# One key-query product per head and chunk, transposed by VectorE and DMA, in a gated recurrence with a feed-forward layer behind it

## The chip, the cores and the metric

The kernel runs on one core of a Trainium2 chip. Its five engines follow their own instruction lists and wait for each other through semaphores: TensorE (PE, with its weight loads listed as PEld), VectorE (DVE), ScalarE (ACT), GpSimd (POOL) and SyncE (SP), which issues all DMAs here. The metric is the device time of one execution in microseconds (us).

## The reference

Four sequences of 768 steps have 8 heads of 48 channels. A complex gate decays and rotates a 48x48 state for each head, an outer product of key and value is added to its real part, and the query reads it. Heads are then joined to 384 columns, and a feed-forward layer with 2048 hidden columns follows. `w_in` and `w_out` come in float64, everything else in float32.

```python
mag = np.sqrt(a_re * a_re + a_im * a_im)
scale = np.minimum(mag, 0.999) / (mag + 1e-06)
a_re_n, a_im_n = (a_re * scale, a_im * scale)
for t in range(S):
    new_re = ar * S_re - ai * S_im
    new_im = ar * S_im + ai * S_re
    S_re, S_im = (new_re + kv, new_im)          # kv = k[t] outer v[t]
    y[:, :, t] = np.einsum('bhd,bhde->bhe', q[:, :, t], S_re)
...
h = x @ w_in                                     # x: y as (3072, 384)
g = h * (1.0 / (1.0 + np.exp(-h)))
return (g @ w_out)
```

In the inputs `a_re` lies between 0.85 and 0.95 and `a_im` is normal with a deviation of 0.1.

## The kernel before, in words

A gate is written as exp(l + 2 pi i th). With L and TH the running sums of l and th, step s reaches step t with the weight sum over d of q k exp(L[t]-L[s]) cos(TH[t]-TH[s]). Queries and keys are rotated by cos and sin (96 rows for 48 channels) and scaled by exp of sums of l, and a product of the two on TensorE gives the weights.

The sequences are cut into 24 chunks of 128 steps, two chunks to a pair, 12 pairs. The recurrence runs within a chunk in blocks of 64 steps, with a state carried from block to block. So that no scale can overflow, a block's weights come from several levels: `scales` (L341) makes six running sums of l for each head by two matmuls of 384 columns (`lt`), ACT turns them into `z` and `zk` by exp, `scaled` (L357) multiplies them with the transposed queries and keys on DVE, and `weights` (L401 to L418) takes products for the levels (`far`, `mid`, `near`) and puts them together through masks. `transposed` (L327) turns queries and keys by TensorE with copies by ACT and DVE, `state` (L383) updates the state once per block, `output` (L424, L428) reads values and states, and `tokens` (L442) turns the result for the feed-forward layer.

The gates of a pair come in `gates_log` and `gates_angle`: squares, logarithms, exponentials and an arctangent on ACT, with steps on DVE and POOL between. `trig` takes sine and cosine of the phases, and `phases` (L278, L280) sums the angles. These need three loads of ACT's function tables per pair, and `chain` keeps all functions on ACT in the order in which they are given.

The feed-forward layer of a pair of chunks has eight steps: `hidden` (L450, 6 products of 256 columns: h), tanh on ACT, a product on DVE (L455: g) and `result` (L465, 4 products of 384 columns: o). A float32 product appears as two MATMUL instructions in the trace. Weights in float64 are converted on DVE in pieces (L129 to L146) while the first pairs run.

The order of work: `attention(p)` gives the steps of a pair, `feed(p-1)` those of the feed-forward layer of the pair before, and `merge` interleaves the two lists. The tile framework then schedules each engine's list, within what its pools of buffers allow; PSUM has 2 banks for `lt` and `mid`, 3 for the rest of attention, 1 for h, 2 for o. After the last pair's attention one feed-forward layer runs alone.

## Time and profile before

| what | value |
|---|---|
| time of three runs | 1490.67 us median, 1480.78 to 1491.67 |
| span of the profiled execution (no device time of its own is listed; it lies 3.4 us above the median) | 1494.1 us |
| TensorE busy | 1341.6 us, 8592 matmul instructions |
| VectorE busy | 734.3 us |
| ScalarE busy | 487.3 us |
| GpSimd busy | 350.7 us |
| DMA packets | 136418, 42.27 MB |

A row of the groups names a line, an engine, an operation and its shape, then the count, the busy time, the mean duration of one (ns) and the idle time ahead of it with what ended it. A row of the timeline begins with its start and duration in us. A row of the stretches gives the stretch, its length, then busy time and count of PE, PEld, DVE, ACT and POOL, the granted clock of TensorE (1.00 is full), the share of DMA time and GB/s. TensorE's instructions overlap in the trace, so that a mean duration is longer than the spacing of a dense row.

### The profile page before, as it was taken

Reading aid. Unit: us, or ns where it says so; the run is one execution under the profiler, and the core shown is the slowest. Engines: PE = TensorE matmul, PEld = TensorE weight load, DVE = VectorE, ACT = ScalarE, POOL = GpSimd, SP = SyncE. Lnnn points to the kernel's source line nnn. Section 1 sums busy time; section 2 is a strip of 40 time slices with the busy share of each in tenths; the row PEclk is TensorE's granted clock in tenths of the full one; section 3 lists DMA queues with packets and bytes.
Section 4 is the critical chain, followed back from the end, with each engine's and each line's share of the span. In section 5 each row is a group of like instructions: output and inputs, shape, how many; then the busy total and the mean of one; then the engine's idle time right before and its main releaser. Section 6 shows DMA issues by size and latency. Waiting matters only on the chain. (4 is left out here: it accounts for less than half of the span.)

```text
span 1494.1 us, 21231 instructions
## 1 busy us (share of the span) xinstructions
PE 1341.6 (90%) x8592; PEld 937.5 (63%) x8592; DVE 734.3 (49%) x1592; ACT 487.3 (33%) x1009; POOL 350.7 (23%) x390
## 2 busy tenths in 40 slices
PE   1563798489999999999999999989999989999999
PEld 0342566256767666666766766756766756776676
DVE  4978778764444444444344444444344444334321
ACT  4433032303523513613523513513433513313301
POOL 5534011501322402301222311311131311301000
PEclk9975799789999999979999989979999999989979
DMA  5313111310020110110020110110010010000000
GB/s 121 85 50 90 41 43 54 75 37 6 17 49 1 32 33 1 31 29 6 13 52 1 29 36 0 28 32 6 6 38 1 12 30 3 6 12 1 1 11 11
DMA packets 136418, 42.27 MB, mean 28 GB/s; under 512 B 126080, under 2 KB 133248, under 8 KB 136320
## 3 DMA queue, kind: packets, MB, share of 16 engines
q1 hardware_dynamic: 136320, 40.91, 11.8%
q8 instruction: 68, 1.11, 0.3%
q14 instruction: 30, 0.25, 0.1%
HBM read 36.18 MB, written 4.72 MB: 27 GB/s over the span
## 5 line engine op out<-in xcount | busy, mean ns | idle before, releaser
L341 PE MATMUL lt<-sums,l 128*96 128x384 f32 x768 | 304.4, 518 | 46.5 <-DVE w L417 30.3
L465 PE MATMUL o<-w,g 128*128 128x384 f32 x768 | 282.2, 499 | 24.3 <-DVE w L146 24.3
L450 PE MATMUL h<-xT,w 128*128 128x256 f32 x1152 | 284.2, 392 | 18.1 <-DVE g L455 15.3
L450 PEld LDWEIGHTS h<-xT,w 128*128 128x128 f32 x1152 | 221.3, 196 | 78.1 <-DVE g L455 19.5
L220 ACT ACTIVATE z<-lt 96x384 f32<-96x384 f32 x384 | 187.2, 488 | 166.1 <-PE lt L341 164.3
L357 DVE TENSOR_TENSOR z<-z,qT 96x256 f32<-96x256 f32 (+1 forms) x288 | 149.4, 530 | 160.0 <-ACT z L220 159.1
L465 PEld LDWEIGHTS o<-w,g 128*128 128x128 f32 x768 | 145.8, 194 | 119.7 <-DVE w L146 27.2
L341 PEld LDWEIGHTS lt<-sums,l 128*96 128x96 f32 x768 | 126.8, 173 | 143.4 <-issue 64.1
L455 DVE SCALAR_TENSOR_TENSOR g<-tanh,h 128x512 f32<-128x512 f32 x96 | 65.3, 680 | 231.5 <-ACT tanh L220 231.5
L432 ACT COPY y<-y 128x192 f32<-128x192 f32 x48 | 15.3, 319 | 399.9 <-PE y L428 399.9
L220 ACT ACTIVATE tanh<-h 128x512 f32<-128x512 f32 x96 | 57.4, 598 | 249.2 <-PE h L450 223.5
L320 POOL TENSOR_TENSOR ks<-kr,es 128x384 f32<-128x384 f32 x48 | 47.5, 1009 | 326.3 <-ACT es L220 326.3
L387 POOL TENSOR_TENSOR S<-S,dec 96x192 f32<-96x192 f32 x88 | 56.1, 647 | 207.9 <-DVE S L390 205.6
L401 PE MATMUL far<-z 96*128 96x128 f32 x384 | 96.2, 334 | 0.1
L424 PE MATMUL y<-v,w 128*128 128x48 f32 x384 | 82.6, 299 | 9.4 <-DVE w L418 9.4
L352 POOL COPY dec<-z 96x8 f32<-96x8 f32 x48 | 32.8, 684 | 243.8 <-ACT z L220 243.8
L424 PEld LDWEIGHTS y<-v,w 128*128 128x128 f32 x384 | 64.0, 202 | 38.1 <-DVE w L418 23.8
L383 PEld LDWEIGHTS s<-v,ks 64*96 64x96 f32 x704 | 59.0, 170 | 41.0 <-issue 36.4
L357 DVE TENSOR_TENSOR z<-z,kT 96x256 f32<-96x256 f32 x192 | 79.7, 415 | 0.0
L410 PE MATMUL near<-z,zk 96*128 96x128 f32 x384 | 61.8, 313 | 14.4 <-DVE S L390 14.2
L300 POOL COPY l<-l 128x768 f32<-128x768 f32 x24 | 37.1, 1545 | 154.9 <-PE lt L341 153.0
L390 DVE TENSOR_TENSOR S<-s,S 96x192 f32<-96x192 f32 x88 | 30.9, 351 | 85.1 <-PE s L383 57.6
(92 smaller groups left out, 1685.2 us busy)
## 6 DMA issues: line engine op xcount, KB each, us to landing
raw<-in_moe_w_in_dram SPq DMA_DIRECT2D x24, 256.0 KB, 2.8
raw<-in_moe_w_out_dram SPq DMA_DIRECT2D x32, 192.0 KB, 2.4
re<-in_a_re_dram SPq DMA_DIRECT2D x24, 192.0 KB, 3.6
im<-in_a_im_dram SPq DMA_DIRECT2D x24, 192.0 KB, 3.3
k<-in_k_dram SPq DMA_DIRECT2D x24, 192.0 KB, 2.6
q<-in_q_dram SPq DMA_DIRECT2D x24, 192.0 KB, 2.7
v<-in_v_dram SPq DMA_DIRECT2D x24, 192.0 KB, 2.7
out_dram<-ot SPq DMA_DIRECT2D x24, 192.0 KB, 1.9
```

The costliest lines, as they stand in the source:

```text
L220: chain(nc.scalar.activation(out=out, in_=in_, func=func, **kw))
L320: nc.gpsimd.tensor_tensor(out=x["ks"][:, :, a], in0=x["kr"][:, :, a], in1=e, op=ALU.mult)
L341: nc.tensor.matmul(ps.rearrange("p s t -> p (s t)"), lhsT=two, rhs=sums[:, ts(g, NS // 2)].rearrange("p s t -> p (s t)"), start=True, stop ...
L357: eng.tensor_tensor(out=t, in0=t, in1=by, op=ALU.mult)
L383: nc.tensor.matmul(ps[:, h], lhsT=x["ks"][rows, hg].rearrange("p a d -> p (a d)"), rhs=x["v"][rows, hg], start=True, stop=True)
L387: nc.gpsimd.tensor_tensor(out=new, in0=x["S", i, hh], in1=x["dec", hh][:, :, ds(i, 1)].to_broadcast([D2, HH, D]), op=ALU.mult)
L401: nc.tensor.matmul(pf[:, h], lhsT=z[:, 2, h], rhs=z[:, 2, h], start=True, stop=True)
L410: nc.tensor.matmul(pn[:, h], lhsT=zk[:, h], rhs=z[:, 0, h], start=True, stop=True)
L424: nc.tensor.matmul(ps[:, h], lhsT=x["w", hh][:, h], rhs=x["v"][:, hh * HH + h], start=True, stop=False)
L450: nc.tensor.matmul(ps[:, ji], lhsT=w1[:, dc, ts(jp * 2 + ji, C)], rhs=A[p]["xT"][:, dc], start=(dc == 0), stop=(dc == ND - 1))
L455: nc.vector.scalar_tensor_tensor(out=g, in0=th, scalar=1.0, in1=ps, op0=ALU.add, op1=ALU.mult)
L465: nc.tensor.matmul(A[p]["o"][m], lhsT=A[p]["g", jp][:, ji, ts(m, C)], rhs=w2[:, j], start=(j == 0), stop=(j == NJ - 1))
```

## The change

The attention is rewritten. The decay of a step is counted from the head row of its chunk of 128: `decays` takes one running sum of l per chunk (a matmul of 384 columns), floors it at -60, and ACT gives exp(L) for queries (`eq`) and exp(-L) for keys (`ek`). `rotated` multiplies these into q and k on POOL and with cos and sin on DVE (`qk`). `turned` transposes on DVE in squares of 32x32 (`sq`), and 12 DMAs per chunk put the squares in their places (`T`; runs of 128 bytes). `weights` is then a single product per head (`a`) and one masked copy on DVE. The levels, their sums, `z`, the masks and TensorE's transposes are gone.

`state` works once per chunk instead of once per 64 steps; the decay over a chunk goes through DRAM (`ends`, `decs`). `output` gives y already transposed, with two heads in the two halves of PSUM's partitions; the last two heads are cut in thirds and sent to their rows by 6 DMAs per chunk (`xT`), for which the rows of `w_in` are permuted on loading. The pairs now go over sequences first (`place`): a pair holds the same chunk of two sequences, and the chunk it follows is two pairs back. Weight conversion uses 6 DVE instructions and a POOL product per piece instead of 9 on DVE, on pieces of 512 (`w_in`) and 384 (`w_out`) columns instead of 256 and 192, all of them listed ahead of the first feed-forward layer. h has 2 banks of PSUM.

For gates too strong for a single product a second path, `step_by_step`, runs the recurrence step by step and the feed-forward layer again. It is behind a branch that is taken when the smallest decay over a chunk is under 4e-18.

```diff
-    BL = 64
-    WC = 256
+    Q = 32
+    NB = D2 // Q
+    NA = C // Q
+    WC = 512
...
+    p_m = fast.enter_context(tc.tile_pool(name="p_m", bufs=2, space=PSUM))
+    p_a = fast.enter_context(tc.tile_pool(name="p_a", bufs=2, space=PSUM))
+    p_h = fast.enter_context(tc.tile_pool(name="p_h", bufs=2, space=PSUM))
+    p_o = fast.enter_context(tc.tile_pool(name="p_o", bufs=2, space=PSUM))
...
+    def place(n):
+        p, i = divmod(n, 2)
+        c, half = divmod(p, B // 2)
+        return 2 * half + i, c
...
+    def load_w1(cols, dc):
+        last = (H - 2) * D
+        third = D // ND
+        rows = [(0, 2 * dc * D, D), (D, last + third * dc, third),
+                (64, (2 * dc + 1) * D, D), (64 + D, last + D + third * dc, third)]
+        load_w(w1[:, dc, ts(cols, WC)], [(at, w_in[r:r + n, ts(cols, WC)]) for at, r, n in rows])
...
+        nc.gpsimd.tensor_tensor(out=x, in0=hi.bitcast(F32), in1=hi.bitcast(F32), op=ALU.mult)
...
+    decs = consts.tile([D2, N, H], F32)
+    ends = nc.dram_tensor("ends", (N, DM), F32).ap()
...
-        ps = bank([C, DM], f"phase{n}")
-        first = n % NCH == 0
-        nc.tensor.matmul(ps, lhsT=upto, rhs=cut(A[p]["th"], i), start=True, stop=first)
-        if not first:
-            nc.tensor.matmul(ps, lhsT=last, rhs=X[n - 1]["turn"], start=False, stop=True)
+        th = cut(A[p]["th"], i)
+        if place(n)[1] > 0:
+            carry = att.tile([1, DM], F32, tag="carry", name=f"carry{n}", bufs=1)
+            nc.sync.dma_start(out=carry, in_=X[before(n)]["turn"][C - 1:C])
+            nc.gpsimd.tensor_tensor(out=th[0:1], in0=th[0:1], in1=carry, op=ALU.add)
+        ps = p_m.tile([C, DM], F32, tag="m", name=f"phase{n}")
+        nc.tensor.matmul(ps, lhsT=upto, rhs=th, start=True, stop=True)
...
+    def decays(n):
...
+        ps = p_m.tile([C, DM], F32, tag="m", name=f"L{n}")
+        nc.tensor.matmul(ps, lhsT=upto, rhs=cut(A[p]["l"], i), start=True, stop=True)
+        L = att.tile([C, DM], F32, tag="whole", name=f"L{n}", bufs=1)
+        nc.vector.tensor_scalar(out=L, in0=ps, scalar1=L_MIN, scalar2=None, op0=ALU.max)
+        for name, scale in (("eq", 1.0), ("ek", -1.0)):
+            x[name] = att.tile([C, DM], F32, tag=name, name=f"{name}{n}")
+            special(x[name], L, AF.Exp, scale=scale)
+        nc.sync.dma_start(out=ends[n:n + 1], in_=x["eq"][C - 1:C])
+        for a in range(2):
+            nc.sync.dma_start(out=decs[a * D:(a + 1) * D, n],
+                              in_=ends[n].rearrange("(h d) -> d h", d=D))
+    def rotated(n):
+        x = X[n]
+        x["qk"] = att.tile([C, 2, H, 2, D], F32, tag="qk", name=f"qk{n}")
+        for w, name in enumerate(("q", "k")):
+            e = x["e" + name]
+            nc.gpsimd.tensor_tensor(out=e, in0=x[name].rearrange("p h d -> p (h d)"), in1=e,
+                                    op=ALU.mult)
+            nc.vector.tensor_tensor(
+                out=x["qk"][:, w], in0=heads(e).unsqueeze(2).to_broadcast([C, H, 2, D]),
+                in1=x["cs"], op=ALU.mult)
+    def turned(n):
+        x = X[n]
+        sq = att.tile([C, NB, 2 * H, Q], F32, tag="sq", name=f"sq{n}", bufs=1)
+        x["T"] = att.tile([D2, 2 * H, NA, Q], F32, tag="T", name=f"T{n}")
+        nc.vector.transpose(sq, x["qk"].rearrange("p w h c d -> p (w h) (c d)").rearrange(
+            "p g (b i) -> p b g i", i=Q))
+        for b in range(NB):
+            for a in range(NA):
+                nc.sync.dma_start(out=x["T"][ts(b, Q), :, a], in_=sq[ts(a, Q), b])
+        T = x["T"].rearrange("p (w h) a j -> p w h (a j)", w=2)
+        x["qT"], x["kT"] = T[:, 0], T[:, 1]
...
+    def weights(n, hh):
+        x = X[n]
+        ps = p_a.tile([C, HH, C], F32, tag="a", name=f"a{n}_{hh}")
+        for h in range(HH):
+            nc.tensor.matmul(ps[:, h],
+                             lhsT=x["kT"][:, hh * HH + h],
+                             rhs=x["qT"][:, hh * HH + h], start=True, stop=True)
+        x["w", hh] = att.tile([C, HH, C], F32, tag="w", name=f"w{n}_{hh}", bufs=3)
+        nc.vector.tensor_tensor(out=x["w", hh], in0=ps,
+                                in1=upto.unsqueeze(1).to_broadcast([C, HH, C]), op=ALU.mult)
+    def output(n):
...
+        v_ = x["v"].rearrange("p h d -> p (h d)")
+        ps = p_m.tile([C, HH, C], F32, tag="m", name=f"y{n}")
+        for hp in range(HH):
+            for r in range(2):
+                h = 2 * hp + r
+                cols = ds(h * D, 64 if h + 1 < H else D)
+                to = ps[64 * r:64 * r + (64 if h + 1 < H else D), hp]
+                carried = "S" in x
+                nc.tensor.matmul(to, lhsT=v_[:, cols], rhs=x["w", h // HH][:, h % HH],
+                                 start=True, stop=not carried)
+                if carried:
+                    nc.tensor.matmul(to,
+                                     lhsT=x["S"].rearrange("p h d -> p (h d)")[:, cols],
+                                     rhs=x["qT"][:, h], start=False, stop=True)
...
+        nc.scalar.copy(out=xT[:, :, ts(i, C)], in_=ps[:, 0:ND])
+        y3 = att.tile([64 + D, C], F32, tag="y3", name=f"y3_{n}")
+        nc.scalar.copy(out=y3, in_=ps[0:64 + D, ND])
+        third = D // ND
+        for r in range(2):
+            for dc in range(ND):
+                nc.sync.dma_start(out=xT[64 * r + D:64 * r + 64, dc, ts(i, C)],
+                                  in_=y3[64 * r + third * dc:64 * r + third * (dc + 1)])
+    def state(n):
+        x = X[n]
+        if place(n)[1] == NCH - 1:
+            return
+        ps = p_m.tile([D2, H, D], F32, tag="m", name=f"s{n}")
+        for h in range(H):
+            nc.tensor.matmul(ps[:, h], lhsT=x["qk"][:, 1, h].rearrange("p c d -> p (c d)"),
+                             rhs=x["v"][:, h], start=True, stop=True)
+        new = att.tile([D2, H, D], F32, tag="S", name=f"S{n + B}", bufs=6)
+        by = decs[:, n].unsqueeze(2).to_broadcast([D2, H, D])
+        if "S" in x:
+            nc.vector.tensor_tensor(out=new, in0=ps, in1=x["S"], op=ALU.add)
+            nc.gpsimd.tensor_tensor(out=new, in0=new, in1=by, op=ALU.mult)
+        else:
+            nc.vector.tensor_tensor(out=new, in0=ps, in1=by, op=ALU.mult)
+        X[n + B]["S"] = new
...
+        if p + 1 < NP:
+            for n in (2 * p + 2, 2 * p + 3):
+                decays(n)
...
+        work = []
+        for n in (2 * p, 2 * p + 1):
+            work += [lambda n=n: weights(n, 0), lambda n=n: state(n), lambda n=n: weights(n, 1),
+                     lambda n=n: output(n)]
+        return work
+    def ahead(p):
+        work = []
+        if p + 1 < NP:
+            for n in (2 * p + 2, 2 * p + 3):
+                work += [lambda n=n: load_x(n)]
+            work += [lambda p=p: gates(p)]
+            for n in (2 * p + 2, 2 * p + 3):
+                work += [lambda n=n: rotated(n), lambda n=n: turned(n)]
+            if p + 2 < NP:
+                work += [lambda n=n: phases(n) for n in (2 * p + 4, 2 * p + 5)]
+        if p + 3 < NP:
+            work += [lambda p=p: load_a(p + 3)]
+        return work
...
+    for p in range(NP + 1):
+        lists = []
+        if p < NP:
+            lists += [attention(p), ahead(p)]
         if p == 0:
-            loads = [lambda s=s: load_w1(s) for s in range(DF // WC)] + [lambda: load_w2(0)]
-            merge(work, loads)
+            lists.append([lambda s=s, dc=dc: load_w1(s, dc) for s in range(DF // WC) for dc in range(ND)]
+                         + [lambda j=j: load_w2(j) for j in range(NJ)])
         else:
+            lists.append(feed(p - 1))
+        merge(*lists)
+    low = consts.tile([D2, 1], F32)
+    nc.vector.tensor_reduce(out=low, in_=decs.rearrange("p n h -> p (n h)"), op=ALU.min,
+                            axis=mybir.AxisListType.X)
+    lows = consts.tile([1, D2], F32)
+    nc.sync.dma_start(out=lows, in_=low)
+    lowest = consts.tile([1, 1], F32)
+    nc.vector.tensor_reduce(out=lowest, in_=lows, op=ALU.min, axis=mybir.AxisListType.X)
+    weak = consts.tile([1, 1], I32)
+    nc.vector.tensor_scalar(out=weak, in0=lowest, scalar1=LEAST, scalar2=None, op0=ALU.is_ge)
+    fast.close()
+    ok = nc.values_load(weak[0:1, 0:1], min_val=0, max_val=1)
+    with tc.If(ok < 1):
+        step_by_step(ctx, tc, q, k, v, a_re, a_im, w1, w2, out)
+def step_by_step(ctx, tc, q, k, v, a_re, a_im, w1, w2, out):
...
+        with tc.For_i(0, S, G) as at:
...
+                tt(tm[0], st[0], on_d("re"), ALU.mult)
+                tt(tm[1], st[1], on_d("im"), ALU.mult)
+                tt(tm[2], st[1], on_d("re"), ALU.mult)
+                tt(tm[3], st[0], on_d("im"), ALU.mult)
+                tt(st[0], tm[0], tm[1], ALU.subtract)
+                tt(st[1], tm[2], tm[3], ALU.add)
+                tt(tm[0], on_d("k"), ins["v"][:, g].unsqueeze(1).to_broadcast([C, D, E]), ALU.mult)
+                tt(st[0], st[0], tm[0], ALU.add)
+                tt(tm[1], st[0], on_d("q"), ALU.mult)
+                nc.vector.tensor_reduce(out=y[:, g], in_=tm[1].rearrange("p d e -> p e d"),
+                                        op=ALU.add, axis=mybir.AxisListType.X)
...
+            with tc.For_i(0, S, C) as at:
...
```

How the work is now ordered is shown at three places. The first is TensorE within one feed-forward layer in the steady part, before (h_2, h_3 and o belong to the feed-forward layer, lt and s to the attention of the next pair):

```order
L450 MATMUL h_2_5512<-xT_5150,w_106 128x256 x6
L341 MATMUL lt_1_0_0_5525<-sums,l_12_5398 96x384
L341 MATMUL lt_1_0_1_5529<-sums,l_12_5398 96x384
L465 MATMUL o_0_5479<-w_107,g_1_5456 128x384
L341 MATMUL lt_1_1_0_5532<-sums,l_12_5398 96x384
L341 MATMUL lt_1_1_1_5536<-sums,l_12_5398 96x384
L465 MATMUL o_0_5479<-w_107,g_1_5456 128x384
L341 MATMUL lt_1_2_0_5539<-sums,l_12_5398 96x384
L341 MATMUL lt_1_2_1_5543<-sums,l_12_5398 96x384
L465 MATMUL o_1_5480<-w_107,g_1_5456 128x384 x2
```

and now, from h_4 on (a, s and phase are all the attention that stands between h_4 and o of g_3):

```order
L383 MATMUL h_4_2146<-xT_1754,w_106 128x256 x6
L321 MATMUL a_0_2166<-T_1818 128x128 x4
L366 MATMUL s_2203<-v_1617,qk_1794 96x48 x8
L321 MATMUL a_1_2239<-T_1818 128x128 x4
L254 MATMUL phase_2229<-th_2045,upto 128x384
L398 MATMUL o_0_1986<-w_107,g_3_2093 128x384 x2
L398 MATMUL o_1_1987<-w_107,g_3_2093 128x384 x2
L383 MATMUL h_5_2173<-xT_1754,w_106 128x256 x6
L398 MATMUL o_0_1986<-w_107,g_4_2155 128x384 x2
```

The products of 384 columns that made the level sums are gone, and the feed-forward products stand closer together.

The second place is ScalarE, where the gate functions of a later pair stand between two tanh of a feed-forward layer. Before:

```order
L220 ACTIVATE mag_5016<-mag_5016 128x768
L217 ACT_TABLE_LOAD
L220 ACTIVATE cos_5033<-cos_5033,half_pi_b 128x384
L220 ACTIVATE sin_5034<-turn_4551 128x384
L220 ACTIVATE cos_5038<-cos_5038,half_pi_b 128x384
L220 ACTIVATE sin_5039<-turn_4568 128x384
L220 ACTIVATE mag_5016<-mag_5016 128x768
L217 ACT_TABLE_LOAD
L220 ACTIVATE tanh_6_5146<-h_6_5139 128x512
```

and now (mag is the arctangent here, eq and ek the two exponentials of a chunk's decays; two table loads and eight functions of the gates stand ahead of this piece, behind tanh_2):

```order
L192 ACTIVATE cs_1668<-abs_1669,half_pi_b 128x8x48
L192 ACTIVATE cs_1668<-turn_1498 128x8x48
L352 COPY y_6_1756<-y_1737 112x128
L192 ACTIVATE cs_1673<-abs_1674,half_pi_b 128x8x48
L192 ACTIVATE cs_1673<-turn_1529 128x8x48
L192 ACTIVATE mag_1651<-mag_1651 128x768
L189 ACT_TABLE_LOAD
L192 ACTIVATE eq_1688<-L_1686 128x384
L192 ACTIVATE ek_1690<-L_1686 128x384
L192 ACTIVATE eq_1699<-L_1697 128x384
L192 ACTIVATE ek_1701<-L_1697 128x384
L192 ACTIVATE tanh_3_1724<-h_3_1717 128x512
```
The block has grown by the four exponentials, and the tanh behind it is that of step 3.

The third place is SyncE's queue over a pair in the steady part. Before it holds loads and the result:

```order
L96 DMA k_5676<-in_k_dram 128x8x48
L96 DMA q_5678<-in_q_dram 128x8x48
L96 DMA k_5693<-in_k_dram 128x8x48
L96 DMA q_5695<-in_q_dram 128x8x48
L88 DMA re_6155<-in_a_re_dram 128x8x48 x2
L471 DMA out_dram<-ot_0_5309 128x384
```

and now, from the decays of one pair to the result of the pair before:

```order
L286 DMA decs<-ends 48x8x1 x2
L251 DMA carry_1890<-turn_1170 1x16x24
L107 DMA k_1956<-in_k_dram 128x8x48
L286 DMA decs<-ends 48x8x1 x2
L107 DMA q_1958<-in_q_dram 128x8x48
L312 DMA T_1765<-sq_1764 32x16x32 x12
L356 DMA xT_1754<-y_7_1921 16x128 x6
L405 DMA out_dram<-ot_0_1939 128x384
L312 DMA T_1818<-sq_1817 32x16x32 x12
L405 DMA out_dram<-ot_1_1942 128x384
```

24 transposing DMAs, 12 for xT and 6 for the decays have come into the queue of each pair, and xT stands behind the T of the next pair's first chunk.

More of the change, by code (lines that the diff above doesn't have):

```diff
@@ L312, in key_state @@
+    def output(n):
         p, i = divmod(n, 2)
         x = X[n]
-        ps = bank([C, DM], f"suffix{n}")
-        nc.tensor.matmul(ps, lhsT=after, rhs=cut(A[p]["l"], i), start=True, stop=True)
-        e = att.tile([C, H, D], F32, tag="es", name=f"es{n}", bufs=1)
-        special(e.rearrange("p h d -> p (h d)"), ps, AF.Exp)
-        x["ks"] = att.tile([C, H, 2, D], F32, tag="ks", name=f"ks{n}")
-        for a in range(2):
-            nc.gpsimd.tensor_tensor(out=x["ks"][:, :, a], in0=x["kr"][:, :, a], in1=e, op=ALU.mult)
```

379 lines of the change are left out of this document (133 added, 246 removed).

## The prediction

> **What bounds the kernel now.** The page comes first: TensorE is busy in nine tenths of the span, VectorE in half of it.
>
> ```profile
> span 1494.1 us, 21231 instructions
> PE 1341.6 (90%) x8592; PEld 937.5 (63%) x8592; DVE 734.3 (49%) x1592; ACT 487.3 (33%) x1009; POOL 350.7 (23%) x390
> ```
>
> Since a busy share is a mean over stages, the stretches come next: two periods in the middle, then three from the last 65 us (stretch, length, then busy time of PE, PEld, DVE, ACT, POOL, then the clock).
>
> ```profile
> 486.00:598.00 112.00, 107.46 (x719) 74.97 (x718) 48.67 (x91) 39.61 (x83) 26.06 (x28) 0.97 0.11 22
> 598.00:710.00 112.00, 107.48 (x690) 74.86 (x688) 49.12 (x91) 39.39 (x82) 24.07 (x26) 0.91 0.10 22
> 1430.00:1440.00 10.00, 9.35 (x92) 7.73 (x91) 2.39 (x4) 0.32 (x1) 0.00 (x0) 0.61 0.05 20
> 1440.00:1450.00 10.00, 9.17 (x38) 7.05 (x39) 0.67 (x2) 0.32 (x1) 0.00 (x0) 0.53 0.01 2
> 1460.00:1470.00 10.00, 10.00 (x40) 7.37 (x39) 1.38 (x2) 1.12 (x2) 0.00 (x0) 1.00 0.00 0
> ```
>
> In the steady part TensorE is busy for 107.5 of 112 us, and every other engine for less than half: TensorE's own work sets the pace. The chain that ended last gives the spacing of its products without waits, and two lines tell where a pair begins and ends: the first h, the copies of the results (ot, first and last), and the copy of the last pair but one.
>
> ```profile
> 1415.66 1.29 PE lt L341 x4
> 1467.64 2.59 PE h L450 x12
> 1470.23 2.58 PE o L465 x8
> ```
> ```profile
> L450 PE MATMUL h<-xT,w x1152: 377/379/797, 184.8 to 1485.4; 128*128 128x256 f32 x192
> L470 ACT ACTIVATE ot<-o x24: 491/491/493, 323.9 to 1490.9; 128x384 f32<-128x384 f32 x24
> 1427.55 0.49 ACT L470 ACTIVATE ot<-o 128x384 f32<-128x384 f32 x1 [8.14 <-PE o L465]
> ```
>
> So the kernel is a start of 323.9 us up to the first pair's result, ten periods of (1427.55 - 323.9)/10 = 110.4 us, a last feed-forward layer of 63.4 us, and 3.2 us to the end of the span. A feed-forward layer costs 8 x (2.59 + 2.58) = 41.4 us of TensorE; the level sums (64 instructions per pair) 16 x 1.29 = 20.6 us; the other 48 us of a period are the rest of attention, slow clock and small waits.
>
> **TensorE's work after the change.** The feed-forward layer keeps its 41.4 us. The new attention is priced by the nearest rows: 8 instructions of 128 columns, 8 of 48 columns on 96 weights, 4 of 48 columns on 64 weights.
>
> ```profile
> 1425.16 1.06 PE L410 MATMUL near<-z,zk 96*128 96x128 f32 x8
> 1420.75 0.88 PE L383 MATMUL s<-v,ks 64*96 64x48 f32 x8
> 166.27 0.32 PE L428 MATMUL y<-S,z 96*64 96x48 f32 x4
> ```
>
> Per pair, a has 16 products (32 instructions): 4 x 1.06 = 4.2 us. s has 16: 4 x 0.88 = 3.5 us. y has 32 products of 64 weights and 128 columns: the trace has none, and its 64 instructions lie between 0.08 us (0.32/4) and 0.133 us (1.06/8), so 5.1 to 8.5 us; I take 0.12, near the upper row, because the columns are the same 128: 7.7 us. Phases and L are 4 products of 384 columns at 1.29/2 = 0.65: 2.6 us. Together 59.4 us, where TensorE is now busy for 107.5 of 112. Transposes, masks, `lt`, `far`, `mid` go with nothing in their place on TensorE.
>
> The clock takes its part: 0.97 and 0.91 in the steady stretches, and 0.61 and 0.53 where short products stand alone. I add 4%, between the two steady rows: 61.8 us. The Trainium skill (TensorE: Matmul & The Clock Gate, Part 1) has the clock halved after an idle window of about 3.4 us; the rows agree only in part, since at 0.53 TensorE was 92% busy, and by that rule the wait below would add an estimated 1.7 us to each of nine periods, 945 us in place of my 930.
>
> **The block of gates on ScalarE.** ScalarE keeps its order of functions, so the tanh behind a pair's gates waits for the whole block, and with it g on VectorE and the next o on TensorE. In the list as it now stands the block sits between tanh_2 and tanh_3. Its pieces:
>
> ```profile
> L217 ACT ACT_TABLE_LOAD x37 | 47.5, 1283 | 1.5 <-PEq L577 0.8
> L220 ACT ACTIVATE mag<-mag 128x768 f32<-128x768 f32 x36 | 30.2, 839 | 43.5 <-POOL mag L250 42.4 <-POOL mag L253 0.9
> L220 ACT ACTIVATE cos<-cos,half_pi_b 128x384 f32<-128x384 f32 x24 | 14.6, 607 | 0.1
> L220 ACT ACTIVATE es<-suffix 128x384 f32<-128x384 f32 x24 | 11.7, 488 | 19.5 <-PE suffix L315 19.0 <-DVE turn L285 0.4
> L220 ACT ACTIVATE tanh<-h 128x512 f32<-128x512 f32 x96 | 57.4, 598 | 249.2 <-PE h L450 223.5 <-DVE t L144 16.4 <-DVE t L129 9.2
> L250 POOL TENSOR_TENSOR mag<-mag,s 128x768 f32<-128x768 f32 x12 | 36.4, 3036 | 81.1 <-DVE s L230 81.1
> L248 DVE TENSOR_TENSOR l<-s,s 128x768 f32<-128x768 f32 x12 | 11.5, 957 | 0.9
> L455 DVE SCALAR_TENSOR_TENSOR g<-tanh,h 128x512 f32<-128x512 f32 x96 | 65.3, 680 | 231.5 <-ACT tanh L220 231.5
> ```
>
> From the start of tanh_2: tanh 0.6; table 1.28; two squares 1.7; VectorE's sum 1.0; four functions 3.4; two VectorE steps to POOL's operand 1.5; POOL 3.0; two functions 1.7; table 1.28; four sines 2.3; arctangent 0.84; table 1.28; four new exponentials 4 x 0.49 = 2.0; tanh_3 0.6; g_3 0.7. Sum 23.2 us. Over that time TensorE's list holds o of g_1 2.6, h_3 2.6, o of g_2 2.6, y of one chunk 3.8, h_4 2.6, a 2.1, s 1.8 and a phase 0.65: 18.7, with the clock 19.5 us. TensorE thus waits 3.7 us in each of eight periods. Before, the block hid behind some 50 us more of attention. Bounds: with no contention POOL's step is 2 us and the wait 2.7; with each of six hand-overs between engines held up by 1.5 us it is 13.
>
> **Transposes, xT and SyncE's queue.** These leave TensorE for others. VectorE's transposes of 1536 elements have no row: from 2 x 0.957 = 1.9 us (two copies of 768) to four times that as the far end. I take 2; two a pair stand behind g_4 and g_7, and even 6.4 us would hold up only the g that follows. VectorE's sum per pair comes to about 31 us against 49 in the stretches: off the path. For the queue:
>
> ```profile
> 48.92 0.39 SPq L96 DMA_DIRECT2D k<-in_k_dram  x1
> 7.36 0.98 SPq L96 DMA_DIRECT2D k<-in_k_dram  x1
> out_dram<-ot SPq DMA_DIRECT2D x24, 192.0 KB, 1.9
> q1 hardware_dynamic: 136320, 40.91, 11.8%
> ```
>
> An issue takes 0.39 us in the quiet and 0.98 us in a row of them, so the 56 DMAs of a pair hold SyncE for 22 to 55 us of 67: room enough, with 12 transposing DMAs out in 5 to 12 us. Data: 0.118 x 16 x 1494 us / 136320 is 20.7 ns a packet; 24 x 512 runs of 128 bytes are 12288 packets a pair, 15.9 us on 16 engines. T of the first chunk is asked for half a period after its issue, that of the second behind h_4; neither is late at these prices. xT is nearer: y's copies 0.8 us, six issues 2.4 to 5.9, landing 1.9 (out_dram's row): 5 to 9 us, while TensorE has o of g_7, s, L and a, 6 to 7 us. I take a wait of 1 us at h_0, 0 to 3. The loads queued behind xT are a period ahead of use.
>
> So a period is 61.8 + 3.7 + 1 = 66.5, taken as 67 us.
>
> **The start.** VectorE converts weights here, and gates come between.
>
> ```profile
> 23.05 0.96 DVE L266 SCALAR_TENSOR_TENSOR th<-mag,re 128x768 f32<-128x768 f32 x1
> 33.16 4.27 POOL L250 TENSOR_TENSOR mag<-mag,s 128x768 f32<-128x768 f32 x1 [12.01 <-DVE s L230]
> 59.96 1.10 DVE L129 TENSOR_SCALAR t<-raw 128x256 int32<-128x256 int32 x1
> 70.72 0.28 DVE L129 TENSOR_SCALAR t<-raw 128x256 int32<-128x256 int32 x1
> 70.93 0.41 DVE L140 SCALAR_TENSOR_TENSOR u<-u,t 128x256 f32<-128x256 int32 x1
> 71.26 0.41 DVE L131 SCALAR_TENSOR_TENSOR t<-raw,t 128x256 int32<-128x256 int32 x1
> ```
>
> The first pair's angles stand at 24 us as before; the second pair's follow POOL's step that ends at 37.4, at about 46. VectorE's list then has rotations, a transpose and one piece of weights, to about 60, and the third pair's gates, a chain of 22 us like the block above with VectorE mostly waiting: 82. Two-tensor steps start 0.33 us apart for 256 columns, scalar ones 0.21; for 512 that is 4 x 0.60 + 2 x 0.34 = 3.1 us a piece, 3.9 with POOL in the way (1.10 against 0.28 in the rows). Ten pieces of `w_in` 39, nine of `w_out` 27 (3.0 each), 13 us of other steps: 161, and h_0 at about 165, where it now starts at 184.8. In the first layer seven more pieces and a block of gates come before g_3, at 202; five more steps bring its result to 225 us, against 323.9. Bounds: 195 if pieces run at 3.1 and the gates hide, 260 if loads of 512 KB hold the pieces up.
>
> **The sum.** 225; eight periods of 67, 536; pair 10 has no logarithms and no wait, 61; pair 11 has no state and nothing ahead, (41.4 + 4.2 + 7.7) x 1.04 = 56; the last layer 41.4 with 4 us for xT uncovered, 46; the end 6 us, the 3.2 of before and about 3 for reading the branch's condition (0 to 10). Together 930 us of span, against 1494.1; the runs' median lies 0.2% under the profiled span, so 928 us.
>
> **The rivals.** *Cheaper by cover*: TensorE's column halves run at the lower price, waits vanish, the start takes 200: 200 + 8 x 59 + 57 + 52 + 43 + 5 = 829; 0.14. For it speaks the dense chain at the end of before, against it the block's sum.
>
> *The block of gates sets the period*: hand-overs to VectorE and POOL (ScalarE's 42.4 us of waits for POOL in its row speak for it, the cover of 19.5 us against it) make the wait 13 us, and the start 245: 245 + 8 x 76 + 63 + 57 + 47 + 6 = 1026; 0.20.
>
> *The transposing DMAs become the bound*: at 20.7 ns a packet they hide. If runs of 128 bytes cost more, other traffic staying at 136320 / 12 packets a pair, 14.7 us, they fill the 67 us at (67 - 14.7) x 16 / 12288 = 68 ns. Each further 10 ns adds 7.7 us a period, about 77 us over ten, and the kernel is slower than before from 68 + 10 x 564/77 = 141 ns on, seven times the row's price. At 90 ns the time is 1099. Up to 141 ns 0.04, beyond 0.02. The Trainium skill (VectorE: DVE Perf Modes, The three transpose paths) calls a plain DMA that transposes by strides 19 times slower than the transposing kind when the destination's step is large; nineteen times the row's price would be 302 us a pair and 3700 us in all, but the steps of single elements are done on VectorE here, and no run of before shows such a DMA.
>
> *The change does not do what it says*: the branch is taken. Then 768 steps of ten VectorE steps over 576 elements, at 0.7 us (g's row), add 5.4 ms. With gates of about 0.9 the decay over 128 steps is near exp(-13), far above 4e-18: 0.01.
>
> **The numbers.** The forecast has 0.59 with its own range of 880 to 980. Faster by over 1% (what a measurement here can tell from no change) in all cases but slow DMAs, the branch and some unseen stall: 0.96; within 1% 0.01; slower 0.03. The range of 860 to 1040 takes in half of the cheap case and two thirds of the gates' case, and leaves out 0.07 below and 0.13 above.
>
> **What would show it.** h and o at 2.59 and 2.58 us between waits; a period near 67 us between ot's copies; idle time of o on g of about 4 us a pair that ends with tanh; T's landing within 5 us; h's first start near 165. The prediction is wrong if TensorE is busy in under 80% of the steady part, or if its waits name DMAs.

## The result, and the profile after

The changed kernel takes 944.6 us (median; 943.8 to 948.2) against 1487.1 us (1480.8 to 1491.7), a ratio of 0.636 with a 95% interval of 0.634 to 0.639. The profiled execution has a span of 942.1 us where the prediction had 930. From its page, and of ScalarE's timeline the first copy of a result for five of the pairs, with the second copy of the last:

```profile
span 942.1 us, 9656 instructions
PE 702.8 (75%) x3424; PEld 518.6 (55%) x3424; DVE 431.4 (46%) x587; ACT 264.2 (28%) x409; POOL 161.5 (17%) x144
```
```profile
246.89 0.49 ACT L404 ACTIVATE ot<-o 128x384 f32<-128x384 f32 x1 [0.83 <-PE o L398]
...
791.15 0.49 ACT L404 ACTIVATE ot<-o 128x384 f32<-128x384 f32 x1 [1.49 <-PE o L398]
841.70 0.49 ACT L404 ACTIVATE ot<-o 128x384 f32<-128x384 f32 x1 [0.84 <-PE o L398]
891.07 0.49 ACT L404 ACTIVATE ot<-o 128x384 f32<-128x384 f32 x1 [0.83 <-PE o L398]
935.00 0.49 ACT L404 ACTIVATE ot<-o 128x384 f32<-128x384 f32 x1 [3.27 <-PE o L398]
936.29 0.49 ACT L404 ACTIVATE ot<-o 128x384 f32<-128x384 f32 x1 [0.80 <-PE o L398]
```

Term by term (the last layer up to the second copy, as the prediction counts it):

| | predicted, us | measured, us |
|---|---|---|
| to the first result | 225 | 246.9 |
| eight periods | 8 x 67 = 536 | 8 x 68.0 = 544.3 |
| pair 10 | 61 | 50.5 |
| pair 11 | 56 | 49.4 |
| last feed-forward layer | 46 | 45.2 |
| end | 6 | 5.8 |
| span | 930 | 942.1 |

The sum is close, but the steps that make it are not all right: a period of 68 is the right length for a partly wrong reason, and so in part luck. TensorE's own work is seen where nothing waits (its timeline, start and length):

```profile
536.12 0.45 PE L341 MATMUL y<-w,v 128*64 128x128 f32 x4
...
538.08 2.86 PE L383 MATMUL h<-xT,w 128*128 128x256 f32 x12
540.78 1.06 PE L321 MATMUL a<-T 96*128 96x128 f32 x8
541.67 1.48 PE L366 MATMUL s<-v,qk 128*96 128x48 f32 x16
542.99 1.12 PE L321 MATMUL a<-T 96*128 96x128 f32 x8
```

From start to start a chunk's y takes 1.96 us, half of a 0.89, s 1.32. A pair has 41.4 (feed-forward) + 3.9 + 3.6 + 2.6 + 2.6 (phases and L) = 54.1 us, not 59.4. The other 13.9 us of a period are mostly waits, summed here over the eight periods (engine, line waited for, us, times, longest):

```profile
PE phase L254 <- POOL th L252: 43.2, 5, 14.1
PE s L366 <- ACT y L352: 16.8, 4, 5.2
PE o L398 <- DVE g L388: 12.5, 8, 2.6
PE h L383 <- DMA xT<-y: 0.8, 1, 0.8
```

That is 73.3 us, 9.2 a period in place of 4.7, and only the third line bears the name that the prediction gave. All of the first three are the block of gates (timelines of one period, by engine):

```profile
395.89 0.60 ACT L192 ACTIVATE tanh<-h 128x512 f32<-128x512 f32 x1 [4.57 <-PE h L383]
...
405.66 2.12 POOL L222 TENSOR_TENSOR mag<-mag,s 128x768 f32<-128x768 f32 x1 [21.36 <-DVE s L202]
...
417.00 0.98 POOL L252 TENSOR_TENSOR th<-th,carry 1x384 f32<-1x384 f32 x1
...
417.07 4.58 DVE L298 TENSOR_TENSOR qk<-ek,cs 128x768 f32<-128x768 f32 x1 [0.57 <-POOL ek L296]
...
417.38 1.06 ACT L192 ACTIVATE tanh<-h 128x512 f32<-128x512 f32 x2
...
418.03 1.65 PE L254 MATMUL phase<-th,upto 128*128 128x384 f32 x2 [6.05 <-POOL th L252]
...
421.57 0.67 DVE L388 SCALAR_TENSOR_TENSOR g<-tanh,h 128x512 f32<-128x512 f32 x1
...
422.30 4.44 PE L398 MATMUL o<-w,g 128*128 128x384 f32 x8 [2.62 <-DVE g L388]
```

tanh_2 starts at 395.89 and g_3 ends at 422.24: 26.3 us, 23.2 predicted. TensorE runs out of other work at 411.98, 16.1 us after tanh_2 (19.5 predicted). Its list has a phase ahead of o(g_3), so most of the wait stands at the phase, whose operand comes out of the same block. g_3 does not follow tanh_3 at once either: a rotation (qk) stands ahead of it in VectorE's list, in all eight periods, and g_3 starts 1.4 to 3.6 us after tanh_3 has ended. That rotation takes 4.58 us here with POOL at work all the while, and 0.91 to 0.96 us where POOL is idle. The s lines wait for the bank that y's copy frees, which stands in ScalarE's list behind parts of the block. In the longest period it is the other way round, and the copy holds the block up for 8 us:

```profile
538.20 0.48 ACT L350 COPY xT<-y 128x384 f32<-128x384 f32 x1 [8.29 <-PE y L344]
...
558.23 1.65 PE L254 MATMUL phase<-th,upto 128*128 128x384 f32 x2 [14.12 <-POOL th L252]
```

### The profile page after: what moved, and what is told of

Read it like the earlier page. It is cut to its first block, busy times and chain, and to the rows that moved or that the text cites. A ratio compares the mean times of both kernels' runs of the same rounds, so it can differ in the third digit from the quotient of the medians.

```text
span 942.1 us, 9656 instructions
## 1 busy us (share of the span) xinstructions
PE 702.8 (75%) x3424; PEld 518.6 (55%) x3424; DVE 431.4 (46%) x587; ACT 264.2 (28%) x409; POOL 161.5 (17%) x144
## 4 chain that ended last, share of the span: by engine, by line
PE 57%; DVE 12%; ACT 12%; SPq 5%; issue 5%; POOL 4%; DMA 3%; DVEq 0%; POOLq 0%; ACTq 0%
PE o L398 25%; PE h L383 22%; ACT mag L192 3%; ACT s L192 3%; ACT L189 3%; PE a L321 2%; POOL mag L222 2%; PE s L366 2%; SPq L312 2%; PE y L341 2%; DVE qk L298 2%; ACT cs L192 2%; DVE t L151 2%; PE phase L254 1%; PE y L344 1%
## 5 line engine op out<-in xcount | busy, mean ns | idle before, releaser
L398 PE MATMUL o<-w,g 128*128 128x384 f32 x768 | 283.4, 515 | 16.1 <-DVE g L388 16.1
L321 PE MATMUL a<-T 96*128 96x128 f32 x384 | 57.8, 301 | 74.7 <-DMA T<-sq 74.7
L254 PE MATMUL phase<-th,upto 128*128 128x384 f32 x48 | 31.2, 755 | 99.4 <-POOL th L252 63.9
L321 PEld LDWEIGHTS a<-T 96*128 96x128 f32 x384 | 55.4, 214 | 84.2 <-issue 61.3
L325 DVE TENSOR_TENSOR w<-a,upto 128x512 f32<-128x512 f32 x48 | 32.3, 681 | 59.1 <-PE a L321 59.1
L366 PE MATMUL s<-v,qk 128*96 128x48 f32 x320 | 38.3, 281 | 26.6 <-ACT y L352 18.3
L366 PEld LDWEIGHTS s<-v,qk 128*96 128x96 f32 x320 | 37.1, 198 | 32.2 <-ACT y L352 19.7
L341 PE MATMUL y<-w,v 128*64 128x128 f32 (+1 forms) x384 | 42.2, 294 | 13.1 <-DVE w L325 13.1
L192 ACT ACTIVATE mag<-mag 128x768 f32<-128x768 f32 x36 | 30.2, 838 | 46.9 <-POOL mag L222 46.0
L308 DVE STREAM_TRANSPOSE sq<-qk 128x1536 f32<-128x1536 f32 x24 | 42.4, 1766 | 2.1 <-DMA T<-sq 2.1
L298 DVE TENSOR_TENSOR qk<-ek,cs 128x768 f32<-128x768 f32 x24 | 38.0, 1582 | 9.6 <-POOL ek L296 9.6
```

Source lines behind the costliest of these rows:

```text
L192: chain(nc.scalar.activation(out=out, in_=in_, func=func, **kw))
L254: nc.tensor.matmul(ps, lhsT=upto, rhs=th, start=True, stop=True)
L298: nc.vector.tensor_tensor(out=x["qk"][:, w], in0=heads(e).unsqueeze(2).to_broadcast([C, H, 2, D]), in1=x["cs"], op=ALU.mult)
L308: nc.vector.transpose(sq, x["qk"].rearrange("p w h c d -> p (w h) (c d)").rearrange("p g (b i) -> p b g i", i=Q))
L321: nc.tensor.matmul(ps[:, h], lhsT=x["kT"][:, hh * HH + h], rhs=x["qT"][:, hh * HH + h], start=True, stop=True)
L341: nc.tensor.matmul(to, lhsT=v_[:, cols], rhs=x["w", h // HH][:, h % HH], start=True, stop=not carried)
```

## Experiments

The edits are shown shortened.

**The block of gates.** First, the block cut in two:

```diff
+    work += [gates_1(p)]             # logarithms, then exp's table
     work += [load_x(n) ...]
-    work += [gates(p)]
+    work += [nothing, gates_2(p)]    # sines, arctangent, decays
```


> Theory: the block of gates on ScalarE sets the period; TensorE runs out of work while the block keeps tanh_3 back (9 us of wait a period, and a slow clock behind it). Cut in two, with tanh_1 to tanh_3 between the halves and one table load more (1.28 us), the first half is a chain of about 15 us and the second of about 10 us, each against 13 us of other products: the spacing of the ot copies falls from 68 to 58 to 62 us, and the time from 945 to 870 to 895 us. Rival (the transposing DMAs, SyncE's queue or VectorE set the period): the spacing stays at 67 or more, and the time lies between 940 and 960 us.

917.2 us (913.3 to 923.9). Faster than the change by 27 us, less than expected: six of the eight spacings are 63 to 64 us, the others 67 and 72. The phase no longer waits in these periods (5.1 us over the whole run), but o waits for g in 16 places, 59.2 us in all: the half with the logarithms still holds tanh_1 back for longer than TensorE has other work.

Next, y's two copies:

```diff
-        nc.scalar.copy(out=xT[:, :, ts(i, C)], in_=ps[:, 0:ND])
+        nc.vector.tensor_copy(out=xT[:, :, ts(i, C)], in_=ps[:, 0:ND])
```
(and the same for `y3`)

> The two copies of y for each chunk go from ScalarE to VectorE. Theory: in two of the eight periods (74.7 and 73.1 us against 65 to 68) ScalarE stands 8 us in the middle of the block of gates because its list has y's copy there and y is not ready; in others s waits up to 5 us for the bank that y's copy frees behind the block. With the copies on VectorE all eight spacings are 63 to 67 us, 915 to 930 us. Rival (the long periods come from something else): two periods stay above 72 us and the time is 940 to 950 us.

939.4 us (938.9 to 941.7), 5 us less and not the time that the theory gave: the waits of s for y's copy go (0.9 us left of 18.3), but one spacing of 74.0 us stays and the others are 63 to 68. In the long period ScalarE waits no more for y; there TensorE's list has more of attention ahead of h_0, so that less lies beside the block, and the phase waits 9.8 us:

```profile
558.22 1.65 PE L254 MATMUL phase<-th,upto 128*128 128x384 f32 x2 [9.81 <-POOL th L252]
```

So moving the copies moves the wait and does not shorten the block.

Then the block in four pieces, with tanh free to run between them:

```diff
+        special(s1, re, AF.Square); special(s2, im, AF.Square); ...   # early, any table
-        magnitude(s1, re)
-        nc.gpsimd.tensor_tensor(out=mag, in0=mag, in1=s1, op=ALU.add)
+        magnitude(s1, re)             # no longer behind l's last step
+        nc.vector.tensor_tensor(out=mag, in0=mag, in1=s1, op=ALU.add)
...
-        table("trig_and_small")       # sines, arctangent
+        table("silu_and_others")      # sines, and tanh
+        table("sigmoid_and_others")   # arctangent, and tanh
```


> The block of gates in four pieces: the squares ahead of the logarithms, |a| + |re| on VectorE and no longer behind POOL, the sines and the arctangent under tables that hold tanh too (one table load more than after has). From tanh_1 to g_2 the chain is then 0.6 + 1.28 + 4 x 0.84 + 1.2 + 1.7 + 1.28 + 0.6 + 0.7 = 10.7 us, against o, h, o, h of 10.3 us and pieces of attention. Theory (the chain of gates is all that keeps a period above TensorE's own work, which is 50.5 us in the pair without logarithms and about 2.6 us more with phases and L): the spacing of ot falls to 53 to 58 us, 825 to 870 us in all. Rival (with the gates out of the way another wait takes over at once: VectorE, SyncE's queue, xT): the spacing stays above 61 us, 890 us or more.

838.1 us (836.6 to 839.3), ratio to the kernel before 0.562 (0.558 to 0.566). The spacings alternate between 55 and 59 to 60 us, the first result comes at 225.6. A stretch of one period (us, then busy time of PE, PEld, DVE, ACT, POOL, clock):

```profile
355.00:410.00 55.00, 54.92 (x314) 41.62 (x314) 22.82 (x31) 16.94 (x28) 9.64 (x9) 1.00 0.30 48
```

In this shorter one TensorE is busy throughout at full clock, near the 54.1 us that its products need. Over the eight periods its waits fall from 73.3 to 12.1 us. So the block of gates is shown to be what a period waited for: it was worth 107 us, 21 of them in the start. How much of that the tables bring and how much the step that left POOL for VectorE, this run doesn't separate.

**The clock behind a wait.**

```diff
+        if i == 0 and 4 <= n:
+            for _ in range(9):
+                nc.tensor.matmul(ps, lhsT=upto, rhs=w1[:, 0, 0:DM], start=True, stop=True)
         nc.tensor.matmul(ps, lhsT=upto, rhs=th, start=True, stop=True)
```


> Nine more products of 384 columns (5.8 us at 0.65 us each, their result is written over) stand in TensorE's list ahead of the first phase of each pair from the third on, so that TensorE is busy where it waited for th. If idle time is what slows the next products: the phase falls from 1.65 to 0.8 us for its two instructions, the eight instructions of o behind it from 4.4 to 5.5 us to about 2.8 us, some 2 to 3 us in each of eight periods: 920 to 930 us. If the clock hangs on something else: no gain, and in the periods with a wait shorter than 5.8 us a loss of 1 to 2 us: 945 to 960 us.

969.5 us (967.5 to 971.2), outside both expectations, because the framework answers the longer list with another order: from the third spacing on they are 68 to 79 us. In the first two the order from h_4 on is kept (parts of a stand elsewhere), and there the gain is seen: 62.9 and 62.4 us against 65.3 and 68.0. After, then filled, at the same place:

```profile
283.79 1.65 PE L254 MATMUL phase<-th,upto 128*128 128x384 f32 x2 [4.95 <-POOL th L252]
287.11 5.46 PE L398 MATMUL o<-w,g 128*128 128x384 f32 x8 [1.68 <-DVE g L388]
```
```profile
286.44 6.07 PE L256 MATMUL phase<-w,upto 128*128 128x384 f32 x18 [0.74 <-DVE S L374]
292.35 0.81 PE L257 MATMUL phase<-th,upto 128*128 128x384 f32 x2
294.20 2.85 PE L401 MATMUL o<-w,g 128*128 128x384 f32 x8 [1.05 <-DVE g L391]
```

With TensorE kept busy the products behind the wait are 0.8 + 2.6 = 3.4 us shorter. The rule of the Trainium skill that the prediction weighed (TensorE: Matmul & The Clock Gate, Part 1) agrees in kind: idle time is paid again in slow products. Its window of about 3.4 us does not: in the run in pieces an o after 2.42 us of idle time took 4.54 us, and the granted clock behind it is 0.50 (a timeline row, then a stretch).

```profile
423.87 4.54 PE L404 MATMUL o<-w,g 128*128 128x384 f32 x8 [2.42 <-DVE g L394]
```
```profile
424.80:428.20 3.40, 3.40 (x6) 1.68 (x6) 1.06 (x2) 3.35 (x5) 0.00 (x0) 0.50 0.55 73
```

**The transposes.** Three kernels: each transposing DMA twice; the same number of packets in one more DMA a chunk; transposes on TensorE.

```diff
+                nc.sync.dma_start(out=again[n, ts(b, Q), :, a], in_=sq[ts(a, Q), b])   # 12 a chunk
```


> Each transposing DMA is issued a second time, to a place in DRAM that nobody reads: 12288 packets of 128 bytes more for each pair, and 24 issues more on SyncE (about 15 us at 0.63 us). Theory (they hide behind TensorE's work): the spacing of ot grows by less than 2 us, 945 to 965 us. Rival (the transposing DMAs are the bound, or close to it): the spacing grows by the 13 to 15 us that the packets or the issues take, 1080 us or more.


```diff
+        nc.sync.dma_start(out=again[n, :, :, 0:Q], in_=sq.rearrange("p b g i -> p (b g) i"))  # 1 a chunk
```


> As many more packets as in the run with each transposing DMA issued twice (12288 of 128 bytes a pair), but in one issue a chunk: sq once more as a whole to a place in DRAM that nobody reads, in runs of 128 bytes. Theory (what cost 146 us there were 24 more issues on SyncE, which has one list and waits in order): 2 issues more a pair, the spacing of ot grows by less than 3 us, 945 to 975 us. Rival (the packets themselves are the load): the time lies near that run's, 1060 us or more.

1090.5 us (1088.1 to 1093.9) and 1015.7 us (1014.5 to 1017.1). The first is what its rival gave (1080 or more); the second lies between its theory and its rival. In both, spacings alternate: 66 us, and 94 or 82 to 84; the long ones hold the y of three chunks and the short ones that of one. SyncE's and TensorE's timelines in a long one of the doubled DMAs, then SyncE's in a long one of the other run (with the shortest, the median and the longest of its twelve issues in ns):

```profile
360.61 8.45 SPq L313 DMA_DIRECT2D T<-sq  x12
369.10 6.66 SPq L316 DMA_DIRECT2D again<-sq  x10
375.88 3.96 SPq L360 DMA_DIRECT2D xT<-y  x6
```
```profile
370.85 3.75 PE L325 MATMUL a<-T 96*128 96x128 f32 x16 [2.96 <-DMA T<-sq]
380.02 7.28 PE L387 MATMUL h<-xT,w 128*128 128x256 f32 x24 [5.43 <-DMA xT<-y]
```
```profile
337.95 12.50 SPq L313 DMA_DIRECT2D T<-sq  x12
```
```profile
L313 SPq DMA_DIRECT2D T<-sq x12: 620/627/5106, 338.0 to 349.8; - x12
```

With more packets alone the twelve issues take 12.5 us in place of 8.0, and a waits for T. The growth is one issue of 5.1 us; the others stay at 0.63. It is seen in four of the 24 chunks, and with the doubled DMAs no issue of T takes more than 1.6 us. With the issues too, xT stands in SyncE's list behind copies that nobody needs, and h_0 waits for it. These are not all the waits of the two stretches (TensorE's: us, times, longest; the doubled DMAs first):

```profile
PE phase L255 <- POOL th L253: 16.4, 2, 10.5
PE h L387 <- DMA xT<-y: 5.4, 1, 5.4
PE a L325 <- DMA T<-sq: 3.0, 1, 3.0
```
```profile
PE phase L255 <- POOL th L253: 9.8, 1, 9.8
PE a L323 <- DMA T<-sq: 6.8, 1, 6.8
```

Of the phase's 16.4 us, 5.9 are for a `carry` that stands behind the doubled copies in SyncE's list. The other 10.5, and the 9.8 of the second run, are the block of gates, which in both runs also costs o 10.6 us in each short spacing. In the long ones a stands ahead of h_0 in TensorE's list. On the mean a spacing grows by 12.2 and 6.6 us, and 34 and 19 us are lost before the first result. How much of the loss is the traffic and how much the order that the framework chose for it, these runs don't separate. What they settle is the margin: the queue is not full (0.49 of the DMA engines' time in the doubled kernel's long stretches), yet as much again costs 71 to 146 us.

> The transposes go back to TensorE (16 of 96 x 128 a chunk, into the banks of a, copied out by VectorE); no stream transpose, no transposing DMAs; all else is the change. Price: 32 x 0.11 us = 3.5 us of TensorE a pair (before shows four in 0.44 us), 8 copies of 0.69 us on VectorE. Theory (the gain came from the level products that went, and the period is set by the gates): part of the 3.5 us lies in the wait, 945 to 985 us. Rival (the gain hangs on transposes that left TensorE, or the banks of a become tight): 1000 us or more.


```diff
-        nc.vector.transpose(sq, ...)
-        ... 12 x nc.sync.dma_start(out=x["T"][ts(b, Q), :, a], in_=sq[ts(a, Q), b])
+        ... 16 x nc.tensor.transpose(ps[0:D2, h], x["qk"][:, w, hh * HH + h], ident)
+        nc.vector.tensor_copy(out=T[:, w, hh * HH:(hh + 1) * HH], in_=ps[0:D2])
```
(T with three buffers, S with five.) 950.5 us (949.4 to 951.3), ratio 0.637 (0.632 to 0.641), not to be told from the change itself. The spacing is 71.6 us, 3.6 more than after, close to the 3.5 us that 32 transposes were priced at, and the first result comes at 221.6 us, 25 earlier. So the DMA transposes as such brought nothing in sum: what they save in the periods they lose in the start. The gain over the kernel before lies in the rest of the change: 77 us of it in the start, and the most of what remains in periods that lost the level products and what served them; no run took these apart. With the gates in pieces, where TensorE hardly waits, transposes on TensorE were not tried.

**The price of y.**

```diff
-        for hp in range(HH):
-            for r in range(2):
+        for r in range(2):
+            for hp in range(HH):
```


> y's products in another order: first those that write partitions 0 to 63, then those that write 64 to 127, in place of taking turns. After shows y at 0.055 us an instruction where a with the same 128 columns takes 0.11. Theory (two products that use different column halves of TensorE run at the same time): y's spacing doubles to 0.11 us, 1.8 us a chunk, of which half lies beside the wait: 945 to 990 us. Rival (64 weights are simply cheaper): spacing stays at 0.055 us and the time at 945 us.

969.3 us (964.3 to 970.5). Four instructions take 0.22 us in after and two take 0.22 us here, and pairs 10 and 11, which don't wait, grow by 2.6 us each (after, then this run):

```profile
508.67 0.44 PE L341 MATMUL y<-w,v 128*64 128x128 f32 x4
508.89 0.44 PE L344 MATMUL y<-T,S 96*64 96x128 f32 x4
```
```profile
315.20 0.38 PE L341 MATMUL y<-w,v 128*64 128x128 f32 x2
315.42 0.38 PE L344 MATMUL y<-T,S 96*64 96x128 f32 x2
```

Products into partitions 0 to 63 and into 64 to 127 run side by side when they take turns. The Trainium skill says so of narrow products at different tile positions (TensorE: Matmul & The Clock Gate, Part 3), and the runs agree: 0.055 against 0.11 us an instruction. The weights are 64 wide in both orders, so that the rival (64 weights are simply cheaper) is wrong. The row of before behind the prediction's lower bound took such turns as well; the prediction read it by its length, 0.32 us for four, where the next row starts 0.25 us later:

```profile
1404.37 0.32 PE L428 MATMUL y<-S,z 96*64 96x48 f32 x4
1404.62 0.42 PE L424 MATMUL y<-v,w 128*128 128x48 f32 x2
```

**The start.** VectorE converts the weights, and the timeline of after shows an L151 with POOL idle and a piece with POOL at work (POOL's row from its own timeline):

```profile
78.42 0.69 DVE L151 SCALAR_TENSOR_TENSOR t<-raw,t 128x512 int32<-128x512 int32 x1
...
95.80 0.43 DVE L149 TENSOR_SCALAR t<-raw 128x512 int32<-128x512 int32 x1
96.26 1.41 DVE L151 SCALAR_TENSOR_TENSOR t<-raw,t 128x512 int32<-128x512 int32 x1
...
100.30 0.42 DVE L149 TENSOR_SCALAR t<-raw 128x512 int32<-128x512 int32 x1
```
```profile
95.93 1.19 POOL L148 TENSOR_TENSOR x<-raw 128x512 f32<-128x512 f32 x1 [3.34 <-DVE w L159]
```

Three kernels change it: one makes both edits on after, one the first edit and one both on the run in pieces:

```diff
-        nc.gpsimd.tensor_tensor(out=x, in0=hi.bitcast(F32), in1=hi.bitcast(F32), op=ALU.mult)
+        nc.scalar.activation(out=x, in_=hi.bitcast(F32), func=AF.Square)
...
-                         + [lambda j=j: load_w2(j) for j in range(NJ)])
+                         + [lambda j=j: load_w2(j) for j in range(4)])
+        if p == 1:
+            lists.append([lambda j=j: load_w2(j) for j in range(4, NJ)])
```


> Only the start: the square of each weight's high word goes from POOL to ScalarE (idle there), and 12 of the 16 pieces of w_out are converted during the first feed-forward layer in place of before it. Theory (VectorE's conversions set the start, slowed by POOL's multiplication beside them: the step with two operands takes 1.41 us in place of 0.69, and h_0 waits behind pieces that it doesn't need): the piece falls from 4.5 to about 3.8 us, the first result comes at 210 to 225 us in place of 247, and the time is 910 to 925 us. Rival (loads, or squares that stand in ScalarE's list between tanh and gates, take the place): first result at 240 or later, 938 to 960 us.

927.9 us (926.8 to 931.5). Without POOL beside it VectorE's L151 takes 0.69 us, so that part is right, and h_0 starts at 160.9 us in place of 180.4. The first result still comes at 248.5 us, as late as in the rival: 12 pieces and the block of gates now stand in the first layer. Of the 17 us gained, 9 are the first spacing (56.0 us in place of 65.3); the rest lies in later ones, where the order changed too.

> The gates in pieces (the run before at 838 us) and the weights' square on ScalarE in place of POOL, with the order of the conversions as in after. Theory (POOL's multiplication slows VectorE's step beside it by 0.7 us a piece, and 28 pieces lie on the way to the first result): the first result moves from 225.6 to about 207 us, 818 to 828 us in all. Rival (loads or attention of the first pair hold the start, or the squares stand in the way of tanh): first result at 222 us or later, 835 us or more.

> As the run of pieces and square, with 12 pieces of w_out converted during the first feed-forward layer. Theory (VectorE's conversions are the whole of the start, so their order moves the work but not its end): the first result within 5 us of that run. Rival (TensorE's idle time ahead of h_0 is what is lost): first result 10 us or more earlier and as much less in all.

With the gates in pieces, the square alone gives 824.9 us (824.2 to 826.0), a time as expected, though the first result moves by 8 us (217.8) and not by 19. Both edits give 813.5 us (810.7 to 819.4), ratio to the kernel before 0.545 (0.541 to 0.549), the fastest of all: the first result comes no earlier (219.3), as the theory said, but the second follows after 39.3 us, because TensorE has begun the second layer by then. So the theory was right about the first result and wrong in taking it for the end of the start; the rival had the gain (11 us) but not its place.

> As the run of pieces and square, and y's copies on VectorE. Theory (ScalarE has room now, so y's copies hold nothing up): within 5 us of that run. Rival (the spacings that alternate, 55 and 59 us, come from y's copies in ScalarE's list): all spacings at 55 us, 15 us less than that run.

825.3 us (823.7 to 827.7): no gain from y's copies on VectorE, and spacings of 55 and 59 to 60 us still alternate, so that the rival is wrong too. The trace shows where the difference lies: in the long ones o waits for g, 2.7 to 3.2 us, and is slow behind it, in the short ones it never does. In the long ones L, s and a stand together ahead of four pairs of o and h in TensorE's list, in the short ones they stand between them. No run tests that this order is the cause.

## Why the prediction was right, and where it was not

- **Bound of before, and the change's direction**: right. TensorE set the pace, and with the level products gone a period fell from 110.4 to 68.0 us; h and o stayed at 2.59 and 2.58 us between waits, and TensorE is busy in the steady part for 471.6 of 545 us, 87%, at a granted clock of 0.90:

```profile
247.00:792.00 545.00, 471.64 (x2372) 349.29 (x2371) 219.87 (x280) 174.82 (x273) 95.88 (x80) 0.90 0.34 58
```

- **TensorE's work after**: too high by 5.3 us a period. y was taken at 7.7 us "near the upper row" and takes 3.9, below its lower bound of 5.1, because its halves overlap (shown by the run with the other order); s 2.6 for 3.5, a 3.6 for 4.2. Pairs 10 and 11, which don't wait, carry this openly: 17 us too many. The rival "cheaper by cover" had the price right, but its waits did not vanish.
- **The block of gates**: the mechanism was right and shown by the run in pieces; its size was off. Wait of o(g_3) 3.7 us and of xT 1, together 4.7; measured 9.2. The chain was 3 us longer than its sum, mostly the rotation ahead of g_3, to which the sum gave nothing; the cover was 3.4 us shorter, since y and the rest of attention are cheaper; and in two periods ScalarE stood 7 to 8 us in mid-block for y (spacings of 74.7 and 73.1 us). The rival "the block of gates sets the period" named the place, with 13 us.
- **The clock**: 4% of TensorE's work, 2.4 us, was taken; 13.9 - 9.2 = 4.7 us are left for slow products and small gaps, an estimate by difference. Filling showed 3.4 us of it at one wait. The 945 us that the rule would have made comes near the span by luck, since the period's other terms were off.
- **So the period**: -5.3 for work, +4.5 for waits, +2.3 for the clock, and 66.5 (taken as 67) became 68.0. That they nearly cancel is partly luck: cheaper products leave less beside the chain, but the chain's own 3 us and the two long periods have nothing to do with them.
- **Transposes, xT and SyncE**: VectorE's transpose took 1.77 us (2 taken), twelve issues 8 us (5 to 12), xT's wait 0.1 us a period (1). T landed 2.2 to 3.9 us after its issue in the run with doubled DMAs; the trace of after does not list it. The transposing DMAs are not the bound: no wait in the eight periods names T. "Room enough" was too easy: doubling the traffic, by price still far from the 67 us, cost 71 us or more. A sum of occupancy said nothing of the order in a list, neither SyncE's nor the one that the framework then chose for TensorE.
- **The start**: 22 us too short. A piece took 4.5 us, not 3.9, and 3.6, not 3.0: an estimated 19 x 0.6 = 11 of the 15 us by which h_0 was late (180.4 for 165). The rest up to the first result is the block in the first layer, where the phase waited 16 us; "the gates hide" was only in the lower bound.
- **The end**: right in size, 5.8 us for 6, though no row of before gave the 3 us for reading the condition. SyncE read it long before, at 869 us, in 0.7 us; 3.0 us pass at its branch instruction after the last result's issue, and the branch was not taken.

## What to carry to other kernels

When the bound engine's work shrinks, measure the longest chain on an engine with an ordered list against what is left beside it, with every price at its low end too; the chain then decides. Cut such a block where a short, urgent step waits behind it (here by tables that serve both), before shaving further products. Look also at what stands between the chain's end and the product that waits for it, on the other engine's list. Transfers that "fit by bandwidth" still need their place in an ordered queue.

## What was not expected of the hardware

Two narrow products side by side at half the price (0.055 for 0.11 us); VectorE's step with two operands at 1.41 for 0.69 us while POOL multiplies, and a rotation at 4.58 for 0.91 to 0.96 us; slow products after only 2.42 us without work; one DMA issue of twelve that takes 5.1 us in place of 0.63, behind a DMA of 6144 small packets.
